# Attention scores of two slots in one burst, with the eight PSUM banks laid out by hand

## The chip, the cores and the metric

The kernel runs on one core of a Trainium2 chip. A core has TensorE (PE, with its weight loads shown as PEld), VectorE (DVE), ScalarE (ACT), GpSimd (POOL) and SyncE (SP), each with a queue of its own that it works through in order. Matrix products land in PSUM, a memory of 128 partitions and eight banks of 512 float32 columns, from which DVE and ACT read. The metric is the time of one execution in microseconds (us); lower is better. Three runs of the kernel before took 559.7, 560.54 and 560.59 us, the median is 560.54.

## What is computed

Attention for 8 batches x 8 heads, 576 positions of 64 numbers. Every score below its row's maximum minus tau is thrown out ahead of the softmax. The heads' outputs, side by side, are 4608 tokens of 512 numbers, which go through two matrices with a hardswish between them:

```
scores = scale * q @ k.T                      # 576 x 576 for each head
scores = where(scores >= max(scores) - tau, scores, -1e9)
attn   = exp(scores - max) / sum              # softmax along a row
x      = heads of (attn @ v) side by side     # 4608 x 512
h      = x @ w_in                             # 512 -> 2048
g      = h * clip(h + 3, 0, 6) / 6
out    = g @ w_out                            # 2048 -> 512
```

Inputs and output are float32.

## The kernel before

**Slots.** Two heads make a pair, two pairs a quad; there are 16 quads, two for each batch. A quad has nine slots. Slots 0 to 3 and 4 to 7 hold 128 query rows each of both heads of one pair; slot 8 holds the remaining 64 rows of both pairs. So 144 slots are in `queue`, numbered n = 0 to 143 over all quads: in an even quad an even slot has an even n, in an odd quad an odd slot has an even n. The main loop makes one turn for each, and what it issues in a turn stands in that order in each engine's queue (`manual_schedule`: nothing is reordered). Work is staggered: a turn finishes the softmax of the slot before and computes the scores of the slot after.

**One turn**, slot n, in program order:
1. ACT: exponentials of slot n-1, with row sums (`sm_exp`, L294, two instructions, one for each head of the pair).
2. DVE: `sm_max` (L281), two instructions: it copies the scores of slot n from PSUM to SBUF and takes their row maxima. POOL makes the bias of each from it (L284).
3. PE: `mm1` (L357), eight bf16 matmuls of one hardswish item, 256 or 320 tokens wide, into two banks; then the relu of it on ACT (slots 0, 1, 3, 5, L366) or DVE (2, 4, 6, 7, L368), and on DVE the gate (L374) that writes `gbuf`. Not in slot 8. The first such item is there from slot 22 of the queue on.
4. PE: `pe_transpose` (L318) of the probabilities of slot n-2, for odd slots below 21, with a DVE copy (L319). Later slots' probabilities are transposed by DMA.
5. DVE: the reciprocal of the row sums of slot n-1 (L297).
6. PE: a part of `mm2` (L386), four bf16 matmuls of 512 columns; four parts make one tile of 128 tokens, which DVE scales and copies out (L394). One part in a turn, none in slot 3, and a second one once in each quad in slot 0 or 1.
7. ACT: `sm_mask` (L289) of slot n, two instructions.
8. PE: one small product: a transpose of q or k of the quad that comes next (L214, L234), or `av_main` (L327, L330; probabilities times v for 512 rows) in slots 3 and 8, or `av_rest` in slot 4. Its result leaves PSUM by DVE (q, av) or by ACT (k, from slot 22 on, L204). From the third batch on q is transposed by DVE itself (L223).
9. PE: `scores` of slot n+1 (L260, L266 in slot 8), in float32. Each head has 64 numbers, so the two heads lie on two row tiles of the array, 64 x 128, and stream side by side into different banks. A float32 matmul is shown as two, each with a weight load of its own. The 576 keys are two halves of 288 columns.
10. POOL: normalisation of slot n-1 (L302), and the DMAs.

**PSUM before.** Pool `ps_s` has two buffers of two banks for the scores, one for each head, so the scores of slot n+1 use the banks that `sm_max` of slot n reads. `ps_h` (two banks) holds mm1's results or `pe_transpose`; `ps_o` one bank for mm2; `ps_m` one for the small products, which before slot 28 alternate between `ps_o` and `ps_m`. After the last slot a tail works off the remaining mm1 items and mm2 tiles, with `ps_s` as additional buffers (`rest1`, `rest2`).

Of the kernel before, what the change touches and what calls it, by code (L numbers as in the profile page):

```python
# [15 lines left out]
P = 128  # L16
# [5 lines left out]
def kernel(  # L22
# [20 lines left out]
    N1 = 22  # L43
    N2 = 28
    scale = 1.0 / math.sqrt(D)
# [14 lines left out]
    o_pool = ctx.enter_context(tc.tile_pool(name="op", bufs=3))  # L60
    ps_s = ctx.enter_context(tc.psum_pool(name="ps_s", bufs=2))
    ps_h = ctx.enter_context(tc.psum_pool(name="ps_h", bufs=1))
    ps_o = ctx.enter_context(tc.psum_pool(name="ps_o", bufs=1))
    ps_m = ctx.enter_context(tc.psum_pool(name="ps_m", bufs=1))

    ctx.enter_context(tc.manual_schedule())

    nat = {}
# [93 lines left out]
    def warm_up(count):  # L162
        warm = ps_h.tile([P, 2, 512], F32, tag="h", name="warm")
        for _ in range(count):
            nc.tensor.transpose(warm[:, 0, 0:P], identf[:], identf[:])

# [22 lines left out]
    now = -1  # L189
    turn = 0  # L190

    def bank(name):
        nonlocal turn
        turn += 1
        if now < N2 and turn % 2:
            return ps_o.tile([P, 512], F32, tag="o", name=name)
        return ps_m.tile([P, 512], F32, tag="m", name=name)

# [10 lines left out]

    def main_pe(src, pair):  # L210
        ps = bank("tp")
        n = pair % 2
        for t in range(4):
            nc.tensor.transpose(ps[:, t * P:(t + 1) * P], src[:, t, 2 * n:2 * n + 2, :], identf[:])  # L214
        return ps

    def transpose_q(pair):
        nq = nat[pair // 2][0]
        if by_pe(pair):
            ps = main_pe(nq[:, 0:1024].rearrange("p (t h d) -> p t h d", h=4, t=4), pair)  # L220
            return lambda: nc.vector.tensor_copy(out=qT_of(pair)[:, 0:512], in_=ps[:])
        n = pair % 2
        nc.vector.transpose(out=qT_of(pair), in_=nq[:, n * S:(n + 1) * S])  # L223

    def transpose_k(pair):
        ps = main_pe(nat[pair // 2][1], pair)
        return lambda: copy_out(kT_of(pair)[:, 64:576], ps[:])

    def transpose_rest(quad, of_k=True, of_q=True):
        ps = bank("tr")  # L230
        nq, _, kr = nat[quad]
        of_q = of_q and by_pe(2 * quad)
        if of_k:
            nc.tensor.transpose(ps[:, 0:P], kr[:], identf[:])  # L234
        if of_q:
            nc.tensor.transpose(ps[:, P:2 * P], nq[:, 1024:1152], identf[:])

        def evict():
            qT, kT = qkT[quad]
            both = ps[:].rearrange("p (w n t) -> p w n t", n=2, t=64)  # L240
            if of_q:
                nc.vector.tensor_copy(out=qT[:, :, 512:S], in_=both[:, 1])
            if of_k:
                copy_out(kT[0:64, :, S:S + 64], both[0:64, 0])
                copy_out(kT[64:P, :, 0:64], both[64:P, 0])
        return evict

    def keys(pair, a, hf):
        kT = kT_of(pair)
        c0 = 64 * (1 - a) + hf * HALF  # L250
        return kT[a * 64:(a + 1) * 64, c0:c0 + HALF]


    def scores(quad, slot):
        tiles = [ps_s.tile([P, 2, 512], F32, tag="s", name="s") for _ in range(2)]
        for hf in range(2):
            if slot < 8:
                pair, t = 2 * quad + slot // 4, slot % 4
                for a in range(2):
                    nc.tensor.matmul(tiles[a][:, hf, 0:HALF], qT_of(pair)[a * 64:(a + 1) * 64, t * P:(t + 1) * P],  # L260
                                     keys(pair, a, hf), start=True, stop=True)
            else:
                for n in range(2):
                    for a in range(2):
                        pair = 2 * quad + n
                        nc.tensor.matmul(tiles[a][n * 64:(n + 1) * 64, hf, 0:HALF],  # L266
                                         qT_of(pair)[a * 64:(a + 1) * 64, 512:S], keys(pair, a, hf),
                                         start=True, stop=True)
        return tiles

# [3 lines left out]
    def sm_max(sl):  # L274
# [4 lines left out]
        sl.rinv = stat_pool.tile([P, 2], F32, tag="rinv", name="rinv")  # L279
        for i, ps in enumerate(sl.tiles):  # L280
            nc.vector.tensor_scalar(out=sl.s[:, i, :].rearrange("p (a b) -> p a b", a=2), in0=ps[:, :, 0:HALF],  # L281
                                    scalar1=1.0, scalar2=None, op0=Alu.mult, op1=Alu.max,
                                    accum_out=sl.m[:, i:i + 1])
            nc.gpsimd.tensor_scalar(out=sl.bias[:, i:i + 1], in0=sl.m[:, i:i + 1], scalar1=-scale, scalar2=tau,  # L284
                                    op0=Alu.mult, op1=Alu.add)
# [27 lines left out]
    def pe_transpose(sl):  # L313
        ps = ps_h.tile([P, 2, 1024], BF16, tag="h", name="pt")
        ps = ps[:].rearrange("p a b -> p (a b)")[:, 0:2 * S].rearrange("p (c t) -> p c t", t=P)
        pn = sl.pn[:].rearrange("p a b -> p (a b)")
        for c in range(9):
            nc.tensor.transpose(ps[:, c, :], pn[:, c * P:(c + 1) * P], identb[:])  # L318
        return lambda: nc.vector.tensor_copy(out=sl.dst, in_=ps)  # L319


    def av(ps, pair, pT, cols):
        b, hp = divmod(pair, NPAIR)
        vm, vr = vsb[b]
        for c in range(4):
            for a in range(2):
                nc.tensor.matmul(ps[a * 64:(a + 1) * 64, :], vm[:, 2 * hp + a, c * D:(c + 1) * D],  # L327
                                 pT[:, 5 * a + c, cols], start=(c == 0), stop=False)
        for a in range(2):
            nc.tensor.matmul(ps[a * 64:(a + 1) * 64, :], vr[:, a, hp, :], pT[:, 4, cols], start=False, stop=True)  # L330

    def av_main(pair):
        b, hp = divmod(pair, NPAIR)
        if hp == 0:
            xT[b] = x_pool.tile([P, KI, S], BF16, tag="xT", name="xT")
        ps = bank("av")
        av(ps[:], pair, pts[pair], slice(0, 512))
        o0 = 64 if b % 2 else 0
        nc.vector.tensor_copy(out=xT[b][:, hp, o0:o0 + 512], in_=ps[:])  # L339

    def av_rest(quad):
        b, g = divmod(quad, 2)
        ps = bank("ar")
        for n in range(2):
            av(ps[:, n * 64:(n + 1) * 64], 2 * quad + n, ptr[quad], slice(n * 64, (n + 1) * 64))
        o0 = 0 if b % 2 else 512
        nc.vector.tensor_copy(out=xT[b][:, 2 * g:2 * g + 2, o0:o0 + 64],
                              in_=ps[:, 0:P].rearrange("p (a b) -> p a b", a=2))

    def mm1(item, pool=None):
        b, ni, c0, w = item
        hps = (pool or ps_h).tile([P, 2, 512], F32, tag="s" if pool else "h", name="h")
        for n in range(2):
            for ki in range(KI):
# [21 lines left out]

    def mm2_part(bb, mt, part, pool=None):
        if part == 0:  # L380
            if pool:
                o_ps[0] = pool.tile([P, 2, 512], F32, tag="s", name="o")[:, 0, :]
            else:
                o_ps[0] = ps_o.tile([P, d_model], F32, tag="o", name="o")[:]
        for ni in range(part * 4, part * 4 + 4):
# [36 lines left out]
    warm_up(4)  # L422
    evict_q = transpose_q(0)
    evict()
# [5 lines left out]
    for quad in range(NQUAD):  # L430
        for slot in range(NSLOT):
            sl = Slot()
            sl.quad, sl.slot = quad, slot
            sl.on_chip = len(queue) < N1 - 1 and len(queue) % 2 == 1
            queue.append(sl)
    queue[0].tiles = scores(0, 0)

    prev = None
    for n, sl in enumerate(queue):
# [31 lines left out]

        pieces = 0 if slot == 3 else 1
        if slot == 0:
            second = True
        if second and slot < 2 and len(todo2) > 1 and todo2[0][1] == todo2[1][1]:
            pieces, second = 2, False
        for _ in range(pieces):
            if todo2:
# [32 lines left out]
        if n == 0:  # L511
            warm_up(8)
        if n + 1 < len(queue):
            queue[n + 1].tiles = scores(queue[n + 1].quad, queue[n + 1].slot)
        if n < 8:
# [18 lines left out]
    last = NQUAD - 1  # L534
    count = [1, 0]

# [9 lines left out]
    def rest1(item, then):  # L546
        h = mm1(item, pool=ps_s if count[0] % 3 else None)
        count[0] += 1
# [3 lines left out]
    def rest2():  # L552
        while todo2:
            bb, mt, part = todo2.pop(0)
            mm2_part(bb, mt, part, pool=ps_s if count[1] % 3 else None)
            if part == 3:
# [50 lines left out]
```

## Time and profile before

The profile is of one execution, taken on the only core.

| | |
|---|---|
| median of three runs | 560.54 us |
| span of the profiled execution, first to last instruction | 558.7 us |
| granted TensorE clock over the span | 0.996 |
| L281, row maxima on DVE | 288 instructions, mean 752 ns |
| L374, gate on DVE | 128, mean 755 ns |
| L260, score matmuls of slots 0 to 7 | 1024, mean 430 ns |
| L357, mm1 | 1024, mean 287 ns |
| L386, mm2 | 535 recorded, mean 379 ns |
| L327, av | 256 of the main form, mean 393 ns |

The profiled execution's own time is its span and what lies around it; the runs' median stands 1.8 us above the span. Matmuls are pipelined and the ends of their records are modelled, so the mean of a record is longer than the distance from one start to the next, and a stream is read from its starts. A wait is written as "A <- B": A's engine was idle, and B's end released it.

### The profile page before, as it was taken

To read this page: it belongs to the slowest core of one execution; us is meant where nothing else is said; L and a number is where in the kernel's file an instruction comes from. 1 tells how busy PE (TensorE), PEld (TensorE's weight loads), DVE (VectorE), ACT (ScalarE), POOL (GpSimd) and SP (SyncE) were. 2 spreads that over 40 slices of the span, in tenths; PEclk is the share of its full clock that TensorE was granted. 3 is DMA by queue.
4 is the path that set the end of the run, shared out by engine and by line. 5 is a ranking of instruction groups with operands and counts; after the bars stand their busy time and mean duration, and the time that the engine had idled before them with its cause. 6 is when DMAs were issued, how large, how long until landed. Compare 5 with 4: busy or idle time off the path is not lost.

```text
span 558.7 us, 11624 instructions
## 1 busy us (share of the span) xinstructions
PE 530.6 (95%) x3829; PEld 309.2 (55%) x3870; DVE 424.7 (76%) x1041; ACT 469.7 (84%) x999; POOL 305.3 (55%) x646
## 2 busy tenths in 40 slices
PE   8899798799999999999999999999999999999997
PEld 6655455555555555655555555655555565654663
DVE  3787686787878788887978788887978798883440
ACT  4899899798889999899898999899898999984440
POOL 2788878854556555755556555755556555561000
PEclk9999899999999999999999999999999999999999
DMA  5999979976789869978689889977689865454102
GB/s 121 137 120 173 196 128 190 204 142 126 137 158 152 152 136 157 178 149 146 130 148 152 173 131 160 175 147 147 131 145 166 150 144 114 100 109 94 38 20 76
DMA packets 286348, 77.52 MB, mean 139 GB/s; under 512 B 269264, under 2 KB 281808, under 8 KB 286288
## 3 DMA queue, kind: packets, MB, share of 16 engines
q1 hardware_dynamic: 267680, 67.47, 65.3%
q0 software_dynamic: 17408, 8.92, 13.6%
q8 instruction: 30, 0.49, 0.4%
q10 hardware_dynamic: 1200, 0.39, 0.3%
q14 instruction: 30, 0.25, 0.1%
HBM read 36.70 MB, written 9.44 MB: 83 GB/s over the span
## 4 chain that ended last, share of the span: by engine, by line
PE 55%; DVE 11%; ACT 8%; issue 4%; SPq 3%; DMA 2%; POOL 2%; DVEq 0%; POOLq 0%
PE h L357 17%; PE o L386 16%; PE s L260 15%; DVE s L281 5%; PE av L327 3%; ACT s L289 3%; ACT s L294 3%; DMA nq<-in_q_dram 2%; DVE g L374 2%; DVE r L368 2%; ACT r L366 1%; PE s L266 1%; PE tp L214 1%; SPq L310 1%; POOL pn L302 1%
## 5 line engine op out<-in xcount | busy, mean ns | idle before, releaser
L302 POOL TENSOR_SCALAR pn<-s,rinv 128x576 bf16<-128x576 f32 x288 | 211.6, 745 | 133.1 <-DVE rinv L297 57.3
L289 ACT ACTIVATE s<-s,bias 128x576 f32<-128x576 f32 x288 | 206.9, 766 | 36.3 <-POOL bias L284 35.2
L281 DVE TENSOR_SCALAR_CACHE_REDUCE s<-s 128x576 f32<-128x576 f32 x288 | 205.9, 752 | 40.3 <-PE s L260 29.9
L294 ACT ACTIVATE s<-s 128x576 f32<-128x576 f32 x288 | 192.7, 671 | 0.3
L260 PE MATMUL s<-kT,qT 64*128 64x288 f32 x1024 | 169.7, 430 | 5.1 <-DVE s L281 2.8
L357 PE MATMUL h<-xT,w_in_sb 128*128 128x320 bf16 (+1 forms) x1024 | 144.9, 287 | 5.9 <-DVE g L374 5.0
L386 PE MATMUL o<-w_out_sb,g 128*128 128x512 bf16 x535 | 133.5, 379 | 5.2 <-DVE osb L394 3.0
L357 PEld LDWEIGHTS <-w_in_sb 128*128 128x128 bf16 x1024 | 92.1, 97 | 68.9 <-issue 31.9
L374 DVE SCALAR_TENSOR_TENSOR g<-r,h 128x512 bf16<-128x512 f32 (+1 forms) x128 | 96.4, 755 | 41.7 <-ACT r L366 39.9
L260 PEld LDWEIGHTS s<-kT,qT 64*128 64x128 f32 x1024 | 93.7, 186 | 60.9 <-DVE s L281 24.0
L284 POOL TENSOR_SCALAR bias<-m 128x1 f32<-128x1 f32 x288 | 54.4, 189 | 66.6 <-DVE s L281 45.8
L386 PEld LDWEIGHTS <-g 128*128 128x128 bf16 x576 | 55.6, 98 | 57.4 <-issue 9.0
L366 ACT ACTIVATE r<-h,three 128x640 f32<-128x640 f32 (+1 forms) x74 | 54.4, 736 | 20.6 <-PE h L357 19.9
L294 ACT ACTIVATION_READ_ACCUMULATOR s<-s 128x1 f32 x288 | 54.2, 188 | 0.0
L368 DVE TENSOR_SCALAR r<-h 128x512 f32<-128x512 f32 (+1 forms) x54 | 40.5, 751 | 0.0
L394 DVE TENSOR_SCALAR osb<-o 128x512 f32<-128x512 f32 x31 | 21.0, 676 | 21.4 <-PE o L386 21.4
L327 PE MATMUL av<-pT,vm 128*64 128x512 bf16 x256 | 34.6, 393 | 2.0 <-ACT kT L204 2.0
L327 PEld LDWEIGHTS <-vm 128*64 128x64 bf16 x512 | 18.0, 111 | 25.3 <-issue 18.8
L297 DVE RECIPROCAL rinv<-rsum 128x2 f32<-128x2 f32 x144 | 23.0, 160 | 11.3 <-ACT s L294 10.5
L339 DVE CAST xT<-av 128x512 bf16<-128x512 f32 x32 | 21.8, 681 | 6.6 <-PE av L330 6.3
L281 DVE DVE_READ_ACCUMULATOR s<-s 128x1 f32 x288 | 23.9, 83 | 0.0
L266 PE MATMUL s<-kT,qT 64*64 64x288 f32 x256 | 20.1, 415 | 0.7 <-DVE s L281 0.7
(44 smaller groups left out, 241.4 us busy)
## 6 DMA issues: line engine op xcount, KB each, us to landing
km<-in_k_dram SPq DMA_DIRECT2D x64, 128.0 KB, 3.0
out_dram<-osb SPq DMA_DIRECT2D x31, 256.0 KB, 2.4
nq<-in_q_dram SPq DMA_DIRECT2D x96, 72.0 KB, 2.7
vm<-in_v_dram POOLq DMA_DIRECT2D x16, 256.0 KB, 5.6
w_in_sb<-in_moe_w_in_dram POOLq DMA_DIRECT2D x16, 128.0 KB, 4.3
w_out_sb<-in_moe_w_out_dram POOLq DMA_DIRECT2D x16, 128.0 KB, 4.5
pT<-pn SPq DMA_TRANSPOSE x119, 3.4
nq<-in_q_dram SPq DMA_DIRECT2D x14, 128.0 KB, 4.4
```

The source lines that it names most:

```text
L260: nc.tensor.matmul(tiles[a][:, hf, 0:HALF], qT_of(pair)[a * 64:(a + 1) * 64, t * P:(t + 1) * P], keys(pair, a, hf), start=True, stop=True)
L281: nc.vector.tensor_scalar(out=sl.s[:, i, :].rearrange("p (a b) -> p a b", a=2), in0=ps[:, :, 0:HALF], scalar1=1.0, scalar2=None, op0=Alu.m ...
L284: nc.gpsimd.tensor_scalar(out=sl.bias[:, i:i + 1], in0=sl.m[:, i:i + 1], scalar1=-scale, scalar2=tau, op0=Alu.mult, op1=Alu.add)
L289: nc.scalar.activation(out=s, in_=s, func=Act.Prelu, bias=sl.bias[:, i:i + 1], scale=scale, alpha=REJECT)
L294: nc.scalar.activation(out=s, in_=s, func=Act.Exp, accum_out=sl.rsum[:, i:i + 1])
L302: nc.gpsimd.tensor_scalar(out=pn[:, i, :], in0=sl.s[:, i, :], scalar1=sl.rinv[:, i:i + 1], scalar2=1.0, op0=Alu.mult, op1=Alu.mult)
L327: nc.tensor.matmul(ps[a * 64:(a + 1) * 64, :], vm[:, 2 * hp + a, c * D:(c + 1) * D], pT[:, 5 * a + c, cols], start=(c == 0), stop=False)
L357: nc.tensor.matmul(hps[:, n, 0:w], w_in_sb[:, ki, (ni + n) * P:(ni + n + 1) * P], xT[b][:, ki, c0:c0 + w], start=(ki == 0), stop=(ki == KI ...
L366: nc.scalar.activation(out=r, in_=hps, func=Act.Relu, bias=three[:])
L368: nc.vector.tensor_scalar(out=r, in0=hps, scalar1=3.0, scalar2=0.0, op0=Alu.add, op1=Alu.max)
L374: nc.vector.scalar_tensor_tensor(out=gbuf[:, ni:ni + 2, c0:c0 + w], in0=r, scalar=6.0, in1=hps, op0=Alu.min, op1=Alu.mult)
L386: nc.tensor.matmul(o_ps[0], gbuf[:, ni, mt * P:(mt + 1) * P], w_out_sb[:, ni, :], start=(ni == 0), stop=(ni == NI - 1))
```

## The change

All of PSUM becomes one tile `ps` of eight banks, and every user gets fixed columns in it. The scores of a head take 576 columns that run on over a bank's border. For head a=1 the odd slots have columns 128 to 703 (384 in bank 0, 192 in bank 1), the even slots 832 to 1407 (192 in bank 1, 384 in bank 2); head a=0 has the same in banks 3, 4 and 5. So the scores of two slots are held at once, in six banks. The scores of a slot are issued in two parts, "small" (192 keys) and large (384 keys).

At the end of each odd turn n both slot n+1 and slot n+2 are computed in one burst; at the end of an even turn none (but slot 1 at the end of turn 0). In a burst without a slot 8 the order of the parts is: small of n+1 (even), small of n+2 (odd), large of n+2, large of n+1. With a slot 8 it is small and large of n+2, then small and large of n+1.

mm1 writes to banks 5 and 6, the half in bank 6 first. All small products go to bank 2. mm2 has bank 7. `pe_transpose` takes 576 columns from the start of bank 6. mm2's parts are issued two in each even turn and none in an odd one. In the tail mm1 rotates over banks 0-1, 2-3 and 4-5, and mm2 over 6 and 7.

```diff
-    ps_s = ctx.enter_context(tc.psum_pool(name="ps_s", bufs=2))
-    ps_h = ctx.enter_context(tc.psum_pool(name="ps_h", bufs=1))
-    ps_o = ctx.enter_context(tc.psum_pool(name="ps_o", bufs=1))
-    ps_m = ctx.enter_context(tc.psum_pool(name="ps_m", bufs=1))
+    ps_pool = ctx.enter_context(tc.psum_pool(name="ps", bufs=1))
...
+    ps = ps_pool.tile([P, 8, 512], F32, name="ps")
+    ps_flat = ps[:].rearrange("p b c -> p (b c)")
...
+    def bank():
+        return ps[:, 2, :]
...
+    def score_tile(n, a, rows=slice(0, P), k0=0, w=S):
+        c0 = 1536 * (1 - a) + (128 if n % 2 else 832) + k0
+        return ps_flat[rows, c0:c0 + w]
+
+    def score_part(n, small):
+        quad, slot = divmod(n, NSLOT)
+        k0, w = ((384, 192) if small else (0, 384)) if n % 2 else ((0, 192) if small else (192, 384))
+        if slot < 8:
+            pair, t = 2 * quad + slot // 4, slot % 4
+            for a in range(2):
+                nc.tensor.matmul(score_tile(n, a, k0=k0, w=w), qT_of(pair)[a * 64:(a + 1) * 64, t * P:(t + 1) * P],
+                                 keys(pair, a, k0, w), start=True, stop=True)
...
+    def scores(*ns):
+        parts = [(n, small) for n in reversed(ns) for small in (True, False)]
+        if len(ns) == 2 and all(n % NSLOT != 8 for n in ns):
+            parts.insert(0, parts.pop(2))
+        for n, small in parts:
+            score_part(n, small)
...
-        for i, ps in enumerate(sl.tiles):
-            nc.vector.tensor_scalar(out=sl.s[:, i, :].rearrange("p (a b) -> p a b", a=2), in0=ps[:, :, 0:HALF],
+        for i in range(2):
+            nc.vector.tensor_scalar(out=sl.s[:, i, :], in0=score_tile(sl.n, i),
...
-        ps = ps_h.tile([P, 2, 1024], BF16, tag="h", name="pt")
-        ps = ps[:].rearrange("p a b -> p (a b)")[:, 0:2 * S].rearrange("p (c t) -> p c t", t=P)
+        pb = ps_flat[:, 3072:3072 + S].bitcast(BF16).rearrange("p (c t) -> p c t", t=P)
...
-    def mm1(item, pool=None):
+    def mm1(item, hb=HB):
...
-        hps = (pool or ps_h).tile([P, 2, 512], F32, tag="s" if pool else "h", name="h")
-        for n in range(2):
+        hps = ps[:, hb:hb + 2, :]
+        for n in (1, 0):
...
-        pieces = 0 if slot == 3 else 1
-        if slot == 0:
-            second = True
-        if second and slot < 2 and len(todo2) > 1 and todo2[0][1] == todo2[1][1]:
-            pieces, second = 2, False
-        for _ in range(pieces):
+        for _ in range(0 if n % 2 else 2):
...
-        if n + 1 < len(queue):
-            queue[n + 1].tiles = scores(queue[n + 1].quad, queue[n + 1].slot)
+        if n == 0:
+            scores(1)
+        elif n % 2 and n + 2 < len(queue):
+            scores(n + 1, n + 2)
...
-        h = mm1(item, pool=ps_s if count[0] % 3 else None)
+        h = mm1(item, hb=2 * (count[0] % 3))
...
-            mm2_part(bb, mt, part, pool=ps_s if count[1] % 3 else None)
+            mm2_part(bb, mt, part, ob=6 + count[1] % 2)
```

`HB` is 5 and `OB` is 7. `score_part` does slot 8 with four matmuls per part, on 64 x 64 tiles.

## The prediction

> **What bounds the kernel now.** I read the page's busy shares first, then the busy time by stretch, then the timeline of single slots, then the waits. The first line is the page's part 1; the next two are the busy time of each engine (with its instruction count) in a stretch before the hardswish layer has work and in one of the steady middle.
>
> ```profile
> PE 530.6 (95%) x3829; PEld 309.2 (55%) x3870; DVE 424.7 (76%) x1041; ACT 469.7 (84%) x999; POOL 305.3 (55%) x646
> ```
>
> ```profile
> 15.00:80.00 65.00, 57.30 (x442) 34.29 (x442) 50.06 (x137) 58.18 (x129) 52.64 (x110) 0.97 1.03 152
> ...
> 250.00:350.00 100.00, 98.76 (x720) 56.11 (x726) 83.17 (x204) 92.20 (x200) 55.59 (x120) 1.00 0.86 149
> ```
>
> PE is never idle in the middle (98.76 of 100 us); DVE has 17 us of slack in 100, ACT 8. From the start of L281 in one slot to its start in the next, quads 4 to 15 take 377.4 us to the end of the last slot (125.7 to 503.1), so 62.9 per two quads (18 slots), 6.99 per two slots. Quads 0 and 1 take 55.6 together, quads 2 and 3 61.5. The rest is 8.6 us of start and a tail of 55.6.
>
> One slot of the timeline (columns: start, length, engine, line, operation):
>
> ```profile
> 332.06 1.24 PE L260 MATMUL s<-kT,qT 64*128 64x288 f32 x8
> ...
> 333.23 1.05 PE L357 MATMUL h<-xT,w_in_sb 128*128 128x256 bf16 x8
> ...
> 333.42 0.76 DVE L281 TENSOR_SCALAR_CACHE_REDUCE s<-s 128x576 f32<-128x576 f32 x1 [0.42 <-PE s L260]
> ...
> 334.11 0.75 DVE L281 TENSOR_SCALAR_CACHE_REDUCE s<-s 128x576 f32<-128x576 f32 x1
> 334.32 0.69 ACT L366 ACTIVATE r<-h,three 128x512 f32<-128x512 f32 x1 [0.19 <-PE h L357]
> ...
> 334.78 0.08 DVE L281 DVE_READ_ACCUMULATOR s<-s 128x1 f32 x1
> ```
>
> The reader is to see four distances. Scores start to DVE's first maximum: 333.42 - 332.06 = 1.36. First maximum to the end of both: 334.86 - 333.42 = 1.44. mm1 starts on PE ahead of the maximum, beside it. And relu follows mm1's start by 1.09, of which eight matmuls are 0.87. The slot's DVE work after the maxima, where relu is DVE's:
>
> ```profile
> 307.51 0.69 DVE L368 TENSOR_SCALAR r<-h 128x512 f32<-128x512 f32 x1
> ...
> 308.23 0.69 DVE L374 SCALAR_TENSOR_TENSOR g<-r,h 128x512 bf16<-128x512 f32 x1
> 308.84 0.16 DVE L297 RECIPROCAL rinv<-rsum 128x2 f32<-128x2 f32 x1
> ```
>
> Relu to the reciprocal's end: 309.00 - 307.51 = 1.49; in the 320-wide items 302.43 - 300.68 = 1.75. Today the loop from maximum to maximum runs through one slot, and its wait costs PE little:
>
> ```profile
> PEld s L260 <- DVE s L281: 24.0, 61, 1.4
> ...
> PE s L260 <- DVE s L281: 2.8, 5, 0.9
> ```
>
> **What the change removes.** Single records of one scores group start at 304.295, 304.642, 304.884 and 305.127, so a pair of row tiles streams 0.2425 and a slot 0.97; the group lasts 1.24. Going in, the weight load starts 0.10 after the last stream's end and is bare for 0.11; going out, mm1's first matmul comes at 305.563, 0.19 after the scores' stream ended. One change of tile shape and back costs 0.39. The change makes 73 bursts of 144, so 71 x 0.39 = 27.7 us of PE disappear. Some 24 even slots end in av, whose column tiles still need a change before mm1 (0.2 each, 5 us): 23 us are left. The score columns (192 + 384 for 2 x 288), DVE, ACT and POOL instructions and the DMAs are the same in number; nothing moves past SP's or POOL's queues. mm2 stays at nine parts per quad, now two in each even slot. The tail has three h buffers as before and two o buffers for three; o's copy takes 0.67 against 3.5 of matmuls, so PE hides it: 0, at most +2.
>
> **What the change adds** is a longer loop. DVE works in program order, so the maxima of an odd slot (n+2) stand behind relu, gate, reciprocal, output copy and eviction of the even slot (n+1). The next burst needs the odd slot's maxima done (its banks 0, 1, 3, 4), and the even slot's maxima need the burst's last part, even-large. So each two slots contain, one after the other: burst, maxima, the even slot's DVE work, maxima. Count from 0 = end of the odd slot's maxima. Burst starts 0.06 later (the weight load at 37.31 after the read-out that ended at 37.25). First maximum: 0.06 + 1.36 + 0.97 for the second slot's stream = 2.39; both done 3.83.
>
> mm1 meanwhile: the bank 6 half streams from 2.30 to 2.73. The bank 5 half shares its bank with even-large and waits for the first maximum's end, 3.15 + 0.06 = 3.21; it ends at 3.64 (3.75 for 320 columns, 4 x 0.135). This wait of 0.5 is new, and mm2, the small product and the next mm1 are queued behind it. Relu can start 0.2 after, 3.84 on either engine (ACT has ended exp by about 2.9), and the reciprocal ends at 3.84 + 1.49 = 5.33, or 3.95 + 1.75 = 5.70; mean 5.5. mm2's eight matmuls (0.216 each) end at 5.4. An output copy (every second pair) starts at 5.65 and ends near 6.25.
>
> Then the period per pair, maxima of 1.44 included (primes: odd quad):
> - (0,1): 5.5 + 1.44 = 6.94, with output 7.7; mean 7.3.
> - (2,3): DVE as before, but PE has two mm1 (0.97 each), mm2, the k transposes (0.43) and av_main (1.28) between bursts: 8.25.
> - (4,5): av_rest ends on PE at 6.1, its cast at 6.5: 7.95.
> - (6,7): 7.3, and even-large (bank 2), due 1.45 after the end of the maxima, waits for ACT's copy behind two masks, about 1.65: 7.5.
> - (8,0'): no mm1, but av's cast ends near 6.1: 7.55.
> - (1',2') and (5',6'): a DVE transpose of q, 0.69: 8.0, and the 0.2 of a k copy: 8.2 each.
> - (3',4'): av_main ends at 6.7 on PE, its cast at 7.5: 8.95; av_rest's cast then holds bank 2 for 0.45: 9.4.
> - (7',8'): 7.3.
>
> Sum 71.7 against 62.9 now: +8.8 per two quads, six times: **+53**. DVE's work per pair is some 6.3 and ACT's some 6.5, so neither is the bound by its sum; DVE is by its order.
>
> Before slot 22 there is no mm1, but the loop is there too, with two more waits: transposes of an even slot go to bank 2 and wait for its second maximum (3.83), so their copy ends at 5.3 and the pair takes 6.8; and PE's transposes of the odd slot's probabilities need POOL's normalisation (4.1 to 5.6; 1.47 for two) and stand ahead of the burst, which then starts at 6.2 to 6.65; with av 7.4 to 7.5. By slots 6 + 6.8 + 6.65 + 6.8 + 7.5 + 6.8 + 7.5 + 6.8 + 7.4 = 62.3 against 55.6: +7. Quads 2 and 3, half of this kind and half of the other: 68.6 against 61.5, +7.
>
> **What the trace doesn't show** is two slots sharing a bank. Even-small, the burst's first part, touches columns that only the even slot's maxima read. If waits go by columns, it can stream before the odd slot's maxima end: 192 columns of two passes, 0.32, and the entry, 0.16, off eight of nine pairs: 0.48 x 8 x 6 = 23 us less in quads 4 to 15, 5 less before. If they go by bank, nothing. The nearest rows are the waits of L260 today, which hold for a tile of whole banks; so I take the bank, and keep both ends. The Trainium skill, "PSUM — Partial Sum Buffer", section "PSUM bank collisions raise a hardware error", speaks against sharing: it says to guard by bank and quadrant, not by address. By it the sum stays at the bank's end, by addresses it would be 28 lower; no run here shows either yet.
>
> **Sum.** The profiled execution spans 558.7; the median of the three runs is 560.54, 1.8 more, which I take as what lies around the span. 558.7 + 53 + 7 + 7 + 1.8 = 627.5, some 67 over the median. The 23 us of saved switches are not subtracted again: the pair periods are built with the short burst.
>
> **Rivals.**
> - Waits by columns: the same loop with an earlier first part, 627.5 - 28 = 600. For it: the columns of that part overlap nothing that the odd slot reads. Against it: the whole-tile waits of today. In a milder form, DVE's slack covers some of the even slot's work.
> - Faster: the loop doesn't bind, PE stays the bound and cashes the switches, 560.5 - 23 = 537. Its place is the end of the odd slot: the maxima would have to be over when PE is through with two mm1, mm2 and the small products, 6.6 per pair. It decides if the even slot's gate is over about 1 us earlier than I have it, and the evictions fall elsewhere. For it: DVE is idle 17% of the middle. Against it: that idle time is waiting for PE and ACT in a fixed order, and even the barest pair needs 6.94.
> - Worse: PE idles over 1 us a pair, and the granted clock, 0.97 in the stretch where PE has gaps now, falls; or bank 2 and bank 5 hold even-large longer (0.5 more in each of 71 pairs, 35 us): 660.
>
> **How the numbers follow.** Loop by bank 0.65, by columns or mild 0.18, worse 0.06, faster 0.09, no change 0.02. The time predicted is the first's, 627. The range leaves out the faster case and most of the worse one: low 585 (the 600 of columns, and a quarter of the steady +53 off), high 650 (two thirds of the way to the worse case). A measurement of this kernel can tell about 0.2%. Faster 0.09, same 0.02, slower 0.89.
>
> **What would show it.** Right: PE's share falls to about 85% with waits of L260 on DVE L281 and of L357 on DVE L281 (about 0.5 in each even slot) at the top; bursts of 16 matmuls some 2.2 long; two maxima pairs near 8 us per two slots in the middle, with (3',4') the longest. Wrong: PE above 95% in the middle, or an odd slot's maxima that are over while PE still works on the odd slot's mm1 in most pairs; then the loop is not the bound. If the burst starts before the odd slot's maxima end, waits go by columns.

## The result, and the profile after

The changed kernel takes 665.38 us (median of four runs, 662.07 to 668.66) against 560.57: ratio 1.186, interval 1.181 to 1.191. The direction was as forecast. The size was not: 105 us more instead of 67, and 665 lies outside the range of 585 to 650.

The page's part 1 of the kernel after, and the busy time of its engines in the same two stretches (the profiled execution took 663.1 us, its span is 661.3):

```profile
PE 566.5 (86%) x3824; PEld 325.1 (49%) x3870; DVE 426.9 (65%) x1041; ACT 472.8 (71%) x999; POOL 306.7 (46%) x646
```

```profile
15.00:80.00 65.00, 44.21 (x371) 28.65 (x373) 41.93 (x118) 50.30 (x110) 45.95 (x95) 0.98 0.90 137
...
250.00:350.00 100.00, 86.92 (x563) 47.59 (x569) 68.18 (x165) 74.05 (x159) 46.94 (x99) 0.97 0.70 125
```

DVE, ACT and POOL do the same work as before in microseconds (426.9 against 424.7, 472.8 against 469.7, 306.7 against 305.3); they only wait more. PE, which had 1.2 us of gaps in 100 here, now has 13, and its instructions in the later stretch fall from 720 to 563; in the early stretch it falls from 57.30 busy to 44.21. The time was lost everywhere but at the very start: from the first maximum of one quad to that of a later one, quads 0 to 3 take 141.2 us for 117.1, quads 4 to 15 (to the last slot's maximum) 448.7 for 374.0, and what follows 62.6 for 59.0. The forecast had 14, 53 and about 0 more; it became 24, 75 and 3.5.

The waits, longest in total (columns: who waited for whom, us in total, times, the longest). Of them:

```profile
PEld ps L257 <- ACT kT L199: 34.5, 17, 3.7
PE ps L257 <- ACT kT L199: 30.2, 14, 3.4
...
PEld ps L257 <- DVE s L284: 24.7, 59, 1.1
...
PEld ps L257 <- DVE g L376: 12.4, 27, 1.0
...
PE ps L359 <- DVE s L284: 6.4, 21, 0.4
```

L257 are the scores, L284 the maxima, L359 mm1, L376 the gate. Scores and mm1 that wait for the maxima were forecast. Scores that wait for the gate, which reads bank 5, were named only in the worse rival, as a bank that is held longer. The first two lines were not forecast: PE waits 30 us for ACT's copy of the transposed keys (L199). Before, L260 waited 0.5 us for it in all. One such wait, by the order of time, ACT above and PE below (start, length, engine, line):

```profile
405.64 0.59 ACT L199 COPY kT<-ps 128x512 f32<-128x512 f32 x1 [1.08 <-PE ps L209]
406.12 0.69 ACT L297 ACTIVATE s<-s 128x576 f32<-128x576 f32 x1
...
406.80 0.67 ACT L297 ACTIVATE s<-s 128x576 f32<-128x576 f32 x1
...
407.46 1.43 ACT L292 ACTIVATE s<-s,bias 128x576 f32<-128x576 f32 x2
408.80 0.53 ACT L199 COPY kT<-ps 64x128 f32<-64x128 f32 x2
```

```profile
409.09 1.24 PE L257 MATMUL ps<-kT,qT 64*128 64x192 f32 x8 [2.49 <-ACT kT L199]
```

This is the end of slot 7 of an even quad. Its burst computes slot 8 and slot 0 of the next quad, and slot 0 needs the next quad's keys, of which the last 64 were transposed in this very turn. ACT copies them after two exponentials and two masks. The kernel before computed slot 0 only one turn later, when the copies were long done. The same holds at slot 2 of an odd quad, whose burst computes slot 4, the first of the second pair. In quads 4 to 15 there are twelve such places, and PE's waits there are 0.97 to 2.50 us long, 23.5 in all.

That the burst waits by bank, not by columns, shows in a burst of even-small first (VectorE's read-outs of the odd slot's two maxima, then PE's weight loads):

```profile
415.82 0.08 DVE L284 DVE_READ_ACCUMULATOR s<-ps 128x1 f32 x1
...
416.50 0.08 DVE L284 DVE_READ_ACCUMULATOR s<-ps 128x1 f32 x1
```

```profile
415.96 0.29 PEld L257 LDWEIGHTS ps<-kT,qT 64*128 64x128 f32 x2 [0.76 <-DVE s L284]
416.63 1.59 PEld L257 LDWEIGHTS ps<-kT,qT 64*128 64x128 f32 x14 [0.38 <-DVE s L284]
```

Each head's first load comes 0.05 to 0.06 after the odd slot's maximum of that head (415.90 and 416.58), although no column of it belongs to that slot.

### The profile page after: what moved, and what is told of

The parts are those of the page before. It is cut to its first block, busy times and chain, and to the rows that moved or that the text cites. A ratio compares the mean times of both kernels' runs of the same rounds, so it can differ in the third digit from the quotient of the medians.

```text
span 661.3 us, 11632 instructions
## 1 busy us (share of the span) xinstructions
PE 566.5 (86%) x3824; PEld 325.1 (49%) x3870; DVE 426.9 (65%) x1041; ACT 472.8 (71%) x999; POOL 306.7 (46%) x646
## 5 line engine op out<-in xcount | busy, mean ns | idle before, releaser
L305 POOL TENSOR_SCALAR pn<-s,rinv 128x576 bf16<-128x576 f32 x288 | 212.4, 748 | 156.2 <-issue 71.7
L284 DVE TENSOR_SCALAR_CACHE_REDUCE s<-ps 128x576 f32<-128x576 f32 x288 | 205.6, 751 | 111.3 <-PE ps L257 59.9
L292 ACT ACTIVATE s<-s,bias 128x576 f32<-128x576 f32 x288 | 207.3, 768 | 71.8 <-POOL bias L287 71.7
L257 PE MATMUL ps<-kT,qT 64*128 64x192 f32 (+1 forms) x1024 | 186.2, 444 | 43.7 <-ACT kT L199 30.2
L359 PE MATMUL ps<-xT,w_in_sb 128*128 128x320 bf16 (+1 forms) x1024 | 154.9, 291 | 12.9 <-DVE s L284 6.4
L257 PEld LDWEIGHTS ps<-kT,qT 64*128 64x128 f32 x1024 | 103.9, 192 | 99.6 <-ACT kT L199 34.5
L359 PEld LDWEIGHTS <-w_in_sb 128*128 128x128 bf16 x1024 | 95.0, 99 | 85.9 <-issue 61.2
L385 PE MATMUL ps<-w_out_sb,g 128*128 128x512 bf16 x530 | 127.6, 381 | 2.9 <-ACT osb L391 0.7
L376 DVE SCALAR_TENSOR_TENSOR g<-r,ps 128x512 bf16<-128x512 f32 (+1 forms) x128 | 96.4, 754 | 47.8 <-ACT r L368 45.9
L368 ACT ACTIVATE r<-ps,three 128x640 f32<-128x640 f32 (+1 forms) x74 | 54.6, 739 | 62.7 <-PE ps L359 44.6
L329 PE MATMUL ps<-pT,vm 128*64 128x512 bf16 x256 | 34.6, 391 | 9.9 <-DVE s L284 4.5
L370 DVE TENSOR_SCALAR r<-ps 128x512 f32<-128x512 f32 (+1 forms) x54 | 40.7, 753 | 3.0 <-PE ps L359 1.3
L199 ACT COPY kT<-ps 64x128 f32<-64x128 f32 (+1 forms) x55 | 22.7, 413 | 22.0 <-PE ps L209 16.5
L263 PE MATMUL ps<-kT,qT 64*64 64x384 f32 (+1 forms) x256 | 25.4, 460 | 1.7 <-DVE s L284 1.1
```

The costliest lines, as they stand in the source:

```text
L257: nc.tensor.matmul(score_tile(n, a, k0=k0, w=w), qT_of(pair)[a * 64:(a + 1) * 64, t * P:(t + 1) * P], keys(pair, a, k0, w), start=True, st ...
L284: nc.vector.tensor_scalar(out=sl.s[:, i, :], in0=score_tile(sl.n, i), scalar1=1.0, scalar2=None, op0=Alu.mult, op1=Alu.max, accum_out=sl.m ...
L292: nc.scalar.activation(out=s, in_=s, func=Act.Prelu, bias=sl.bias[:, i:i + 1], scale=scale, alpha=REJECT)
L305: nc.gpsimd.tensor_scalar(out=pn[:, i, :], in0=sl.s[:, i, :], scalar1=sl.rinv[:, i:i + 1], scalar2=1.0, op0=Alu.mult, op1=Alu.mult)
L329: nc.tensor.matmul(pb[a * 64:(a + 1) * 64, :], vm[:, 2 * hp + a, c * D:(c + 1) * D], pT[:, 5 * a + c, cols], start=(c == 0), stop=False)
L359: nc.tensor.matmul(hps[:, n, 0:w], w_in_sb[:, ki, (ni + n) * P:(ni + n + 1) * P], xT[b][:, ki, c0:c0 + w], start=(ki == 0), stop=(ki == KI ...
```

## The experiments

Names used below: LOOP (the order of DVE's work), KEYS (the keys a turn too late), CLOCK, PAIRS (two mm2 parts in a turn), SHARE (mm1 and the small products in banks that the scores use). Times are medians; the kernel before, run beside them, stood at 560.2 to 561.2. "Quads 0 to 3" and "quads 4 to 15" are the two stretches of above.

**Keys one turn earlier** (in odd quads q's transposes too, which stand a turn before the keys').

```diff
-        if slot == (1 if quad else 2):
+        if slot == (1 - quad % 2 if quad else 2):
             evict = transpose_q(2 * quad + 1)
-        elif slot == (2 if quad else 3):
+        elif slot == (2 - quad % 2 if quad else 3):
             evict = transpose_k(2 * quad + 1)
...
+        early = quad % 2 == 0 and not by_pe(nxt)
...
                 evict = transpose_q(nxt)
+                if early:
+                    evict = transpose_k(nxt)
             elif slot == 6:
-                evict = transpose_k(nxt)
-            else:
+                evict = transpose_rest(quad + 1) if early else transpose_k(nxt)
+            elif not early:
                 evict = transpose_rest(quad + 1)
```

> Theories on the 105 us that the change costs. LOOP: DVE's program order puts the even slot's relu, gate, output copy and eviction between the two slots' maxima, and the burst waits for the second maxima. KEYS: the burst computes the slot after next, so it needs the transposed keys one turn sooner than before, and ACT's copy of them stands behind two exponentials and two masks (30.2 us of PE waiting on ACT's copy in the trace of the changed kernel). CLOCK: these long waits make the granted clock fall to half for 3.4 us at a time. Here the transposes of q and k of an odd quad's second pair, and those of the next quad's k in the even quads from quad 4 on, are one turn earlier. KEYS: 30 us of waits go, and with CLOCK some 10 us more: 620 to 637, clock over 0.985. LOOP alone: 655 to 668.

630.22 us, ratio 1.1247 (1.1217 to 1.1277). KEYS is worth 35 us, with what it did to the clock. Quads 4 to 15 fall from 448.7 to 418.1, which is 7 more than the 23.5 that PE waited there; over the whole kernel PE's wait for the keys falls from 30.2 to 3.4:

```profile
PE ps L257 <- ACT kT L199: 3.4, 1, 3.4
```

The clock of the steady part is whole again, here in tenths by 40 slices, first after the change, then with the keys early:

```profile
PEclk9999888799998998999987999999998999999999
```

```profile
PEclk9996898899999999999999999999999999999999
```

The mean clock of 0.980 is below the 0.985 that was expected, because of dips in quads 0 to 3, which this edit hardly touches.

**PE kept busy in those waits.**

```diff
+        if n > N1 and slot == (2 if quad % 2 else 7):
+            for _ in range(20):
+                nc.tensor.transpose(ps[:, 0, 0:P], identf[:], identf[:])
```

> The changed kernel with 20 transposes that nobody reads put ahead of the two bursts per two quads that wait for keys, from slot 22 on; they go to bank 0, which the burst writes over. They take 20 x 0.108 = 2.2 us, about the length of the wait. CLOCK: the half-clock stretches of the steady part go, clock over 0.985, 650 to 658. If the clock costs nothing: 665 to 675, whatever the clock does.

661.29 us, ratio 1.179 (1.172 to 1.187), between the two expectations; it overlaps the change's own interval. The half-clock stretches of the steady part went, as the third number from the end shows (the granted clock, first after the change, then with the transposes):

```profile
350.00:450.00 100.00, 89.40 (x602) 50.82 (x613) 68.72 (x169) 74.77 (x162) 47.17 (x99) 0.97 0.70 125
```

```profile
350.00:450.00 100.00, 92.29 (x663) 55.83 (x673) 69.50 (x171) 75.64 (x162) 48.32 (x102) 1.00 0.71 128
```

Quads 4 to 15 took 446.4 for 448.7. That is not the price of the clock, for the transposes have a price of their own. From the first maximum of an odd turn to that of the next odd turn, the five places with a half-clock stretch became 6.9 us shorter in sum, and the seven that wait for keys without one became 4.6 longer. So the slower clock cost some 7 us in quads 4 to 15, or more if the transposes lengthen those five places too. The four runs of this kernel say the same: the two with a mean clock of 0.994 took 657.5 and 658.0, those with 0.978 and 0.981 took 665.4 and 664.6. PE's waits of 23.5 and these 7 make up the 31 that early keys gained there. CLOCK is real, and the smaller part.

**The odd slot's maxima in the even turn.**

```diff
-        sm_max(sl)
+        if n < N1 or n % 2 == 0:
+            sm_max(sl)
...
             mm1_gate(item, h, r)
             todo2.extend(then)
+        if n >= N1 and n % 2 == 0:
+            sm_max(queue[n + 1])
```

> The changed kernel with the odd slot's maxima issued in the even turn before it, directly behind that turn's gate and ahead of its reciprocal, output copy and eviction (from slot 22 on). LOOP: output copies and evictions leave the loop, 61 turns with 0.4 us each on average and some of the av waits: 630 to 645. KEYS alone: 660 to 668.

649.18 us, ratio 1.1576 (1.1541 to 1.1611): 16 us of the 20 to 35 expected. With the keys early as well:

> The changed kernel with both cures, keys one turn earlier (630.2 alone) and the odd slot's maxima in the turn before (649.2 alone). LOOP and KEYS add: 665 - 35 - 16 = 614, and less, since the keys' wait no longer hides the loop: 598 to 615. If the maxima only seemed to be late because of the keys: 625 to 635.

620.32 us, ratio 1.1078 (1.1023 to 1.1132): only 10 below the keys alone, under the gain that the place of the maxima should have had if it were the one bound. The waits of the score loads show where the rest went. With the keys early:

```profile
PEld ps L257 <- DVE s L284: 19.4, 53, 0.8
...
PEld ps L257 <- DVE g L376: 16.3, 34, 1.0
```

With the maxima early as well they wait for the gate instead:

```profile
PEld ps L257 <- DVE g L376: 27.6, 43, 1.2
...
PEld ps L257 <- DVE s L284: 1.7, 6, 0.4
```

**The burst undone, the rest kept.** `scores(n + 1)` at the end of every turn, in the changed banks:

> The changed kernel's banks and mm2 in pairs, but one slot's scores at the end of every turn as before: only the burst is undone. LOOP and KEYS both live in the burst, so both go: 560 to 585, where what is above 560 is mm1's half in bank 5 waiting for the first maximum in even turns (0.25 to 0.5 in 64 turns). If the shared banks are the cost: over 620.

659.03 us, ratio 1.1741 (1.1708 to 1.1773). The expectation failed, and with it the view that LOOP and KEYS, which live in the burst, are the whole cause. Without any burst the kernel is nearly as slow. Its waits point to bank 5: scores wait for the gate that reads it,

```profile
PEld ps L257 <- DVE g L376: 40.6, 44, 1.3
...
PE ps L257 <- DVE g L376: 27.6, 41, 1.0
```

and mm1's second half waits for the maxima (9.3 us, 29 times). So SHARE and PAIRS were added as rivals. mm2 in pairs alone, in the kernel before (`for _ in range(0 if n % 2 else 2)` in place of the old count):

> The kernel before, with mm2's parts two in each even turn and none in an odd one: that part of the change alone. LOOP and KEYS need the burst: 556 to 566. If putting mm2 in pairs starves PE in the odd turns (PAIRS, a rival since the run with single scores and shared banks stayed at 659): over 580.

577.81 us, ratio 1.0315 (1.0292 to 1.0337): 17 us, less than PAIRS asked for and more than nothing. Single scores, mm2 one part per turn, changed banks:

> The changed kernel's banks, but one slot's scores per turn and one part of mm2 per turn, as before. SHARE (bank 5 for mm1 and even slots' scores, bank 2 for small products and scores): the 659 of the run with single scores stays, 630 to 660. PAIRS: the odd turn gets its 0.86 us of PE work back while it waits for maxima and gate: 570 to 600.

629.44 us, ratio 1.1228 (1.1202 to 1.1253): PAIRS costs 30 here, and 69 are left. The same with every slot's scores in banks 0, 1, 3 and 4, so that mm1's banks and bank 2 belong to nobody else:

```diff
-        c0 = 1536 * (1 - a) + (128 if n % 2 else 832) + k0
+        c0 = 1536 * (1 - a) + 128 + k0
...
-        k0, w = ((384, 192) if small else (0, 384)) if n % 2 else ((0, 192) if small else (192, 384))
+        k0, w = (384, 192) if small else (0, 384)
```

> The changed kernel's one PSUM tile with fixed columns, one slot's scores per turn, one mm2 part per turn, and every slot's scores in banks 0, 1, 3, 4, so that nobody shares a bank with mm1 or the small products (629.4 with the sharing). SHARE: the time of the kernel before comes back, 553 to 570. If the layout itself costs (192 + 384 columns, one tile for all, banks crossed by a read): 600 to 630.

562.50 us, ratio 1.0034 (1.0013 to 1.0056). This settles the layout: one tile for all of PSUM, parts of 192 and 384, a read across a bank's border cost 2 us together; the shared banks cost 67, with one slot's scores per turn. How much of it is bank 5 (mm1) and how much bank 2 (small products) was not separated.

**Order and place, with the keys early.** mm2's two parts ahead of mm1 on PE in even turns:

> The changed kernel with keys early (630.2), and in even turns mm2's two parts on PE ahead of mm1, DVE's order unchanged. mm1 then never waits for the first maximum to leave bank 5. SHARE: the 0.25 to 0.5 of that wait go in 54 turns: 605 to 620. LOOP: mm1, relu and gate come 1.3 us later, and the maxima of the odd slot stand behind them: 640 to 690.

689.87 us, ratio 1.2299 (1.2257 to 1.2341): 60 slower than with mm1 first, as LOOP asks, although the even turn's mm1 hardly waits for the maxima any more (3.1 us for 7.5). Of the 60, 53 lie in quads 4 to 15 (418.1 to 471.0). Their even turns have 48 gates, which end 4.48 us after the turn's first maximum instead of 3.11 (means), and the cost is 1.1 for each. The run does not tell LOOP from bank 5, though: the odd turn's mm1 needs the banks that the even gate reads, and PE's wait of mm1 for the gate rose from 5.5 to 57.3. One mm2 part per turn, as before the change:

> The changed kernel with keys early (630.2), and mm2 one part per turn as in the kernel before. PAIRS (which cost the kernel before 17 us and the single-score variant 30): 600 to 615. LOOP says the even turn's output copies partly move behind the odd maxima and av comes 0.86 us sooner: also 605 to 620. If in the burst the place of mm2 doesn't matter: 626 to 634.

630.14 us, ratio 1.1242 (1.1185 to 1.1299): no difference in the time. In the burst the place of mm2 doesn't matter, unlike in the two runs without it. Relu by parity of the turn (`on_act=(n % 2 == 0)`):

> The changed kernel with keys early (630.2), and the relu on ACT in every even turn and on DVE in every odd one (four of eight per quad on each, as before). In odd turns ACT's relu stands behind a mask and an exponential, and the gate of the odd turn holds bank 5 against the burst's last part. If this late gate is a part of the loop: 608 to 622. If not: 626 to 634.

633.88 us, ratio 1.1308 (1.1287 to 1.1329): nothing gained (quads 4 to 15 took 418.7 for 418.1), 4 us worse in all; that theory fell. All four together:

> All four cures together: keys early, odd maxima in the even turn, relu by parity, mm2 one part per turn. LOOP: the period per two slots comes to 7.0 to 7.4, so 575 to 605. If it goes under 560, the burst is worth having; SHARE says it can't, since mm1 and the scores still take turns in bank 5.

650.46 us, ratio 1.1604 (1.1577 to 1.1632): the expectation failed, and it is 30 slower than the first two of them together (620.32). Which of the other two does that beside the early maxima was not tried and stays open. The waits point at mm2's place: mm1 waits 22.0 us for the gate, as it does with one mm2 part per turn and early keys alone (23.8), where with the first two cures it was 3.3; and mm2 waits 17.2 for its output copy.

**Which of LOOP and SHARE bounds the burst.** The next four leave the same work out (and set the columns of `gbuf` that nobody writes to zero once, at the start), so they are read against their control, the first.

```diff
-        for c0, w, mts in (((0, 320, (4, 5, 6)), (320, 256, (7, 8))) if b % 2 else
-                           ((0, 256, (0, 1)), (256, 320, (2, 3)))):
+        for c0, w, mts in (((0, 256, (4, 5, 6)), (320, 256, (7, 8))) if b % 2 else
+                           ((0, 256, (0, 1)), (256, 256, (2, 3)))):
```

The last two of the four also put mm1 into one bank:

```diff
+        if hb == HB:
+            hps = ps[:, 6, :].rearrange("p (n c) -> p n c", n=2)
```

> Control: the kernel before with the same work left out (64 tokens of each batch half). PE is the bound and loses 64 items x 8 x 0.027 = 14 us: 543 to 550.

545.28 us, ratio 0.9737 (0.9722 to 0.9752). Quads 0 to 3 took 115.1, quads 4 to 15 363.1.

> Control with less work: the changed kernel with keys early, and every 320-wide mm1 item cut to 256 columns (64 tokens of each batch half are left out of the hardswish layer, so their output isn't computed). Less work on PE, ACT and DVE in half of the items: 612 to 624.

616.06 us, ratio 1.1003 (1.0972 to 1.1033), 71 over its control: quads 0 to 3 137.6, quads 4 to 15 408.4.

> The same reduced work, but both halves of an mm1 item (2 x 256 columns) lie in bank 6 alone, so mm1 and the scores share no bank; the scores' burst and the order of everything stay. SHARE: bank 5 was the bound of the burst too: 565 to 590. LOOP: the maxima's place is the bound, and only mm1's late half is gained: 598 to 618.

599.42 us, ratio 1.0721 (1.0663 to 1.078): quads 4 to 15 392.7. mm1's shared bank is worth 16 of the 45 us that these quads had over the control, 17 in all: what LOOP allowed, at its lower end, and less than SHARE alone would have.

> The same, with the odd slot's maxima in the even turn too. SHARE and LOOP each hide the other, so only the two cures together free the burst: 540 to 570, near the control of the kernel before. LOOP alone as cause: 585 to 600. Neither: over 600.

575.40 us, ratio 1.0276 (1.0214 to 1.0337), between the two theories' ranges: quads 4 to 15 373.0. With mm1's bank its own, the maxima's place is worth 20 us in these quads, where it was worth 6 with the bank shared (418.1 to 411.9). So the two did hide each other in part. The wait of the score loads for the maxima is gone (the lines of these kernels stand two lower; first with mm1's bank its own, then with the maxima early too):

```profile
PEld ps L259 <- DVE s L286: 23.2, 59, 0.9
```

```profile
PEld ps L259 <- DVE s L286: 1.9, 7, 0.4
```

PE is nearly full again in the steady stretch:

```profile
300.00:400.00 100.00, 96.62 (x720) 59.40 (x730) 80.56 (x204) 91.24 (x199) 58.59 (x123) 1.00 0.87 156
```

Ten us stay over the control in quads 4 to 15, and 17 in quads 0 to 3. For those, bursts only from slot 22 on:

```diff
-        c0 = 1536 * (1 - a) + (128 if n % 2 else 832) + k0
+        c0 = 1536 * (1 - a) + (128 if n % 2 or n < N1 else 832) + k0
...
-        if n == 0:
-            scores(1)
+        if n + 1 < N1:
+            scores(n + 1)
         elif n % 2 and n + 2 < len(queue):
```

> The changed kernel with keys early (630.2), and up to slot 21 one slot's scores per turn in banks 0, 1, 3, 4 as in the run at 562.5; bursts only from slot 22 on. Quads 0 to 3 took 138.9 us with bursts from the start and 117.1 in the kernel before. If the burst's loop is what the early stretch pays, about the 22 slots of 36 come back: 612 to 620. If it is the changed PSUM layout or mm2's place: 627 to 633.

615.09 us, ratio 1.0981 (1.0945 to 1.1017): quads 0 to 3 fall from 138.9 to 123.2, quads 4 to 15 stay at 418.1. The first 22 slots (first maximum of slot 0 to that of slot 22) take 67.4, as in the kernel before, where early keys alone left them at 81.1. But the edit undoes two things there, the burst and the scores' share in bank 2. Without the burst and with bank 2 shared (single scores, 659.03 and 629.44) these slots took 73.9 and 74.7, and 65.9 with single scores in banks of their own. So about half of the early loss is the burst's, and half goes only when the scores leave bank 2.

> The best burst found, with the same late start: reduced work (64 tokens of each batch half left out), mm1 alone in bank 6, keys early, odd maxima early (575.4), bursts from slot 22 on. Control 545.3. If all costs but the burst's own waits are gone: 555 to 563, still above the control; under 545 would mean that the saved switches of tile shape pay once the waits are gone.

563.86 us, ratio 1.0062 (1.0042 to 1.0082), against the control's 545.28: 6.4 more in quads 0 to 3 (121.6), 10.0 more in quads 4 to 15 (373.1), 2.4 after. Even the best burst found is 3% slower than the kernel before at equal work. What the last 10 us of the steady part are was not taken apart. Bank 2 is a candidate that was left untried: it stayed shared in every burst, and without the late start (575.40) score loads in quads 4 to 15 still wait 9.5 us for copies out of it (7.0 for ACT's of the keys, 2.5 for DVE's of av), where the control has no such wait.

## Why the prediction was wrong, point by point

- **The step that failed** is the price of the keys' copy. The forecast let it hold only bank 2, "behind two masks, about 1.65", and charged 0.2 each in "(6,7)" and "(1',2')", 2.4 us in quads 4 to 15. It looked at the copy as something that frees a bank, and not as something whose result the next burst reads. Since the burst computes slot n+2, it reads keys copied in turn n, and ACT comes to the copy only after two exponentials and two masks. Measured: PE waits of 0.97 to 2.50 us in the twelve places, 23.5 in all, and the half-clock stretches beside them, some 7. Taking the waits away gave 31 us in quads 4 to 15, 35 in all. (The 0.2 in "(5',6')", whose burst needs no new keys, was of the right size: a load waits 0.20 there in three of the six.)
- Pair by pair one sees where the step failed. These are, from the timelines, the distances in us from the end of one odd slot's maxima to the next's, means of the six times in quads 4 to 15:

| pair | forecast | after the change | keys early |
|---|---|---|---|
| (0,1) | 7.3 | 7.1 | 7.1 |
| (2,3) | 8.25 | 7.8 | 7.8 |
| (4,5) | 7.95 | 8.6 | 8.6 |
| (6,7) | 7.5 | 7.3 | 7.7 |
| (8,0') | 7.55 | 10.1 | 7.6 |
| (1',2') | 8.2 | 7.8 | 7.1 |
| (3',4') | 9.4 | 11.25 | 8.9 |
| (5',6') | 8.2 | 7.9 | 7.9 |
| (7',8') | 7.3 | 7.55 | 7.55 |
| sum | 71.7 | 75.4 | 70.3 |

- The two pairs that are far off, (8,0') and (3',4'), are those whose burst reads keys that were copied in the same turn. With early keys every pair is within 1.1 of the forecast. The kernel then takes 630 against the 627 forecast, but part of that agreement is luck: quads 4 to 15 are 44 slower for the 53 forecast, quads 0 to 3 22 for 14, the tail 3 for about 0.
- **The loop** was right: maxima, the even slot's gate, maxima, burst. The maxima moved forward (16 us alone, 10 with keys early, 24 with mm1's bank free, where the score loads' wait for them went from 23.2 to 1.9) show that it is one of two bounds close together. The run with mm1 delayed (60 us) fits it, but lengthens both. The other bound is mm1's bank 5, forecast as a wait of 0.5 for the first maximum. That is only half of it: mm1 of the odd turn waits for the gate of the even one, and even-large for the gate of the odd one (16.3 us of the score loads with early keys), so bank 5 has a loop of its own. Freed, it gives 17 us.
- **Waits by bank**, taken over waits by columns, was right, as the weight loads 0.05 to 0.06 after each read-out show. That is what the Trainium skill asks for ("PSUM — Partial Sum Buffer", section "PSUM bank collisions raise a hardware error"), and here the waits of the trace show it in force.
- **The switches of tile shape**: a burst of 16 score matmuls that waits for nothing lasts 2.14 from its first weight load to the next instruction's, two single slots 2 x 1.17 = 2.34, and it has one gap of about 0.2 at its edges where they have two: 0.4 saved a pair, as forecast. The typical burst after the change lasts 2.81, so it waits 0.67 inside, most often for the odd slot's second maximum (the loads at 415.96 and 416.63 above) or for the gate that reads bank 5. That is more than the 0.4 that was saved. The forecast allowed 0.2 to 0.45 in some pairs.
- **The tail** of "0, at most +2" came to 3.5; 2.7 of them are there with single scores in unshared banks as well. Its cause was not looked for.
- **The clock** was a part of the worse rival. It did fall to half in quads 4 to 15, beside waits for keys, and cost some 7 us there or more.
- The faster rival needed the maxima's end 1 us earlier. With the maxima moved forward, mm1's bank free, early keys and a late start, the burst still stood 19 us over its control.

## What to carry to other kernels

Before work is moved a turn ahead, list what it reads as well as what it writes over, and find in each engine's order where the last of those inputs is made: a copy that was off the critical path by a turn can be on it. Here two users of one PSUM bank took turns in it through every engine that reads it (67 us with single scores), so price a shared bank as a loop (write, read, next write) and compare the loop with the period, before the switches or the waits that it saves. If curing one bound gains little, a second one of nearly the same length is likely, and only both cures together show it. When a cure adds work of its own, as the filling transposes did, its total says little: compare the places that had the illness with those that had not.

## What was not expected of the hardware

The granted clock went to half for 3.4 us, or 6.8, in five places of the steady part (from 199.9, 254.5, 333.0, 350.1 and 503.7 us on). Each lies at a wait for keys that left PE idle for 1.4 to 2.5 us: four begin 0.1 to 1.4 us after its end, the one at 350.1 within it. No longer idle time of PE stands near them, and PE was 72 to 85% busy in the 10 us ahead of each. Seven other such waits, of 0.97 to 2.49 us, had no half-clock stretch, so the length of the wait alone does not decide; what does is not shown. Filling the waits with transposes kept the clock at 1.00.
